# Fused attention backward: the core alternates dK with o, dQ and dV of two units, and the output projections move with it

## The chip, the core and the metric

The kernel runs on one core of one Trainium2 chip. Times are device microseconds (us) of one execution, medians over several. TensorE is called PE here, its weight loads PEld, VectorE DVE, ScalarE ACT, GpSimd POOL, and SyncE SP; "SPq" in a profile is SP's sequencer issuing DMAs. Nearly all DMAs of the part studied here are issued from SP, one after the other; I call that the sync queue.

## The reference, cut to what matters

The reference concatenates a linear-attention block and a multi-query attention block and returns the output and the gradients of all eight inputs and weights. The change concerns the attention block alone: sequence 2048, 16 heads of 28, one key and one value head shared by all.

```python
def _B_ref(x, wq, wk, wv, wo):
    q = (x @ wq).reshape(B, S, H, Dh) ...       # B=1, S=2048, H=16, Dh=28
    k = x @ wk;  v = x @ wv
    scores = jnp.einsum("bhqd,bkd->bhqk", q, k) * (Dh ** -0.5)
    p = _softmax(scores, axis=-1)
    o = jnp.einsum("bhqk,bkd->bhqd", p, v)
    return o....reshape(B, S, H * Dh) @ wo
...
_out, _vjp = jax.vjp(_f, ...);  _grads = _vjp(grad_out)
```

## The kernel before

After a first phase (the linear-attention block and projections, to about 245 us) comes a loop of 512 units. A unit is 256 queries by two heads by 256 keys. Eight units make a block (all 2048 keys, for 256 queries and two heads), eight blocks make one turn of 64 units (256 queries, all 16 heads). In unit `u` PE makes the scores S of unit `u` and the gradient products dP of unit `u - 16` (`w`); ACT takes two exponentials (`sp` to `eT`) and one copy of half of dP; DVE and POOL make dS (`dsT`), DVE a 32x32 transpose of it (`dsx`). From these PE accumulates o, dQ (both in the bank `oq`), dK and dV.

dV needs the exponentials with keys and queries exchanged. For that each pair of units issues one DMA transpose of 128x2048 bf16 (`eN<-eT`) on the sync queue. At the end of a block the o of two heads is transposed back on PE and normalised into `onat`. At the end of a turn `onat` is written to `on_d`, one more DMA transpose makes `oTq` of it, and two output projections multiply it by `wo`.

```python
psS = ...tile_pool(name="psS", bufs=3, PSUM)     # score banks, in rotation
psD = ...tile_pool(name="psD", bufs=2, PSUM)
...
def out_proj(i):
    ps = psS.tile([P, 512], F32, name="sps")
    for c in range(4):
        mm(ps[:, 0:D], oTq[i // 2][:, 4 * (i % 2) + c, :], wo[:, c, :], ...)
    ot = flat(R3)[:, 5120:5120 + D]               # one staging buffer
    nc.vector.tensor_copy(out=ot, in_=ps[:, 0:D])
    nc.sync.dma_start(out0[i * P:(i + 1) * P, D:2 * D], ot)
...
for u in range(NU + 28):                          # NU = 512
    if u == 14 or u % 64 == 32 and u < 448:       # qX: 16 DMAs of 64 KB
        for a in range(4):
            for B in range(4):
                nc.sync.dma_start(qx[32 * a:32 * a + 32, B, :, :], qn_d[r0:r0 + 64, :]...)
    ...
    rows_SD(u, sp, dp)                            # S and dP, tiles of 32 x 128
    nc.scalar.activation(out=et[:, u % 2, 0, :], in_=sp[0][:, :], func=ACT.Exp, ...)
    ...                                           # dS on DVE; cp on ACT; dS on POOL
    nc.scalar.activation(out=et[:, u % 2, 1, :], in_=sp[1][:, :], func=ACT.Exp, ...)
    if u % 2 == 1:
        nc.sync.dma_start_transpose(en[:, :, :], et...)                # eN<-eT
    ...                                           # block end, u = 8b+9: transposes into a bank of psS
    # six units of eight: 2 or 3 dK steps, tiles of 32 x 32
    # every unit: o of unit u-1 and dQ of unit u-18, tiles of 128 x 32
    # two units of eight: dV
    ...
    if u % 64 == 1 and u > 1:
        nc.sync.dma_start_transpose(oTq[q_][:, :, :], onat[q_]...)     # unit 65
    if u % 64 in (16, 24) and u > 64:
        out_proj(2 * (u // 64 - 1) + u % 64 // 8 - 2)                  # units 80 and 88
    ...
    if 0 <= y < NU and y % 8 == 7:                # dQ eviction, on ACT
        nc.scalar.activation(out=qT_B[g]..., in_=oq[64:128, 0:256], func=ACT.Copy, scale=scale)
```

## Time and profile before

| kernel before | value |
|---|---|
| median (lowest to highest), first three runs | 1175.03 us (1173.59 to 1176.06) |
| span of the profiled run | 1172.0 us |
| the loop, first score to last exponential | about 245 to 1091 us |
| one block; a block with an output projection | 12.78 us; 13.75 us |
| one turn of 64 units | 104.17 us |

The last two rows are differences between start times of the first exponential (line 710) in ACT's timeline. The page opens with each engine's busy time and share of the span:

```profile
PE 1099.7 (94%) x15388; PEld 444.6 (38%) x15388; DVE 885.5 (76%) x1669; ACT 900.9 (77%) x1788; POOL 699.4 (60%) x835
...
PEclk9999998989999999999999999999999999999999
```

The second line is the clock granted to PE, in tenths over 40 slices of the span; 9 means 90% or more. PE looks like the bound with 94%. But this share does not say what sets the pace of a unit, so units are read one by one. ACT's timeline (start, duration, engine, line, operation, output and input) of parts of two units:

```profile
465.56 0.60 ACT L710 ACTIVATE eT<-sps 128x512 bf16<-128x512 f32 x1
466.05 0.59 ACT L717 ACTIVATE cp<-dps 128x512 bf16<-128x512 f32 x1
466.53 0.61 ACT L720 ACTIVATE eT<-sps 128x512 bf16<-128x512 f32 x1
467.01 0.61 ACT L710 ACTIVATE eT<-sps 128x512 bf16<-128x512 f32 x1
...
468.63 0.38 ACT L847 ACTIVATE R_63<-oq 64x256 bf16<-64x256 f32 x1
469.04 0.60 ACT L710 ACTIVATE eT<-sps 128x512 bf16<-128x512 f32 x1
```

One unit is 1.45 us from first exponential to first exponential: three instructions, each starting 0.49 us after the one before, although each lasts 0.6. There ACT is full. The next unit takes 2.03 us: its block-end transposes had taken a score bank, and the dQ eviction (L847) sits in it. In a block of eight, six units take 1.46 to 1.55 us, one 2.03 and one 1.81.

The second thing to read is the sync queue, which no engine's busy share shows. Its timeline, at two places:

```profile
420.56 9.12 SPq L699 DMA_DIRECT2D qX<-qn_d  x16
429.79 5.70 SPq L723 DMA_TRANSPOSE eN<-eT  x2
...
475.48 1.80 SPq L723 DMA_TRANSPOSE eN<-eT  x1
477.37 1.12 SPq L750 DMA_DIRECT2D on_d<-onat  x1
478.54 1.94 SPq L838 DMA_TRANSPOSE oTq<-onat  x1
480.58 18.62 SPq L723 DMA_TRANSPOSE eN<-eT  x7
```

Each row begins where the one before it ended: SP issues without a pause. The sixteen loads of a qX take 9.1 us of it; eN transposes take 2.66 to 2.85 us each when they follow each other (18.62 us for seven, 5.70 for two). The Trainium skill, page Perfetto Trace Analysis, What "DMA-bound" means, lists an issuing sequencer whose track is solid DMA slices as one way to be DMA-bound, beside busy DMA engines. Here the view by stretches shows both: the packets make up 0.54 of the DMA engines' time while the sixteen loads are issued (420.5 to 429.7 us, 144 GB/s), but 1.21 and 1.16 in the stretches of transposes after it (184 and 191 GB/s; packets overlap, so the sum can pass 1). From 283 to 824 us there is hardly a gap. So an eN transpose is issued late: comparing each issue with the end of the exponential that completes its eT, the lag is 0 to 15 us, jumps by about 9 us at every qX load and is worked off until the next.

The oTq transpose at 478.54 belongs to unit 129 (unit 65 of the cut: the second of its turn), whose first exponential is at 467.01 us. Its reader, the projection of unit 144, is at 491.93 us, so nobody waits. The view of everything that touches the tile oTq says the same, in the line of what ended the idle time of its readers: only "issue", no DMA.

```profile
L79 PE MATMUL sps<-wo,oTq x64: 352/353/363, 387.8 to 1129.8; 128*128 128x448 bf16 x64
L838 SPq DMA_TRANSPOSE oTq<-onat x8: 1291/1298/1960, 374.4 to 1095.8; - x8
its engine sat idle before it (us, times) until:
  issue: 3.2, 15
```

### The profile page before, as it was taken

What the parts mean: (1) busy time and instruction counts of PE and PEld (TensorE: products, weight loads), DVE (VectorE), ACT (ScalarE), POOL (GpSimd) and SP (SyncE); (2) the same over time, 40 slices, a digit from 0 to 9 for tenths busy, and PEclk for the clock granted to TensorE, in tenths of its full rate; (3) what the DMA queues carried; (4) which work ended last, traced back from release to release, by engine and by line L of the source; (5) the groups of instructions that cost most, each with busy time, mean ns of one, the idle gap of its engine ahead of it and who ended that gap; (6) DMA issues with size and microseconds to landing.
All of it is one profiled execution on the core that took longest, in us unless ns stands there. A gap on an engine that the chain in (4) does not pass through costs nothing. (4 is left out here: it accounts for less than half of the span.)

```text
span 1172.0 us, 38434 instructions
## 1 busy us (share of the span) xinstructions
PE 1099.7 (94%) x15388; PEld 444.6 (38%) x15388; DVE 885.5 (76%) x1669; ACT 900.9 (77%) x1788; POOL 699.4 (60%) x835
## 2 busy tenths in 40 slices
PE   7999997988989999999999999999999999999998
PEld 4555543333333333333333333333333333333344
DVE  7886400336889898888889888988999899888922
ACT  3453112357989999999999999999999999999511
POOL 9000150003777777777778777877787778777900
PEclk9999998989999999999999999999999999999999
DMA  9779897059999999999999999999999999999962
GB/s 259 126 130 184 160 188 177 20 125 198 180 179 190 188 164 187 190 184 175 189 188 160 199 188 186 162 198 188 152 195 182 189 170 199 184 168 163 240 147 75
DMA packets 684435, 202.91 MB, mean 173 GB/s; under 512 B 651232, under 2 KB 679392, under 8 KB 684256
## 3 DMA queue, kind: packets, MB, share of 16 engines
q1 hardware_dynamic: 673664, 190.26, 94.8%
q10 hardware_dynamic: 9312, 6.65, 2.1%
q0 software_dynamic: 1280, 3.55, 1.1%
q8 instruction: 120, 1.97, 0.7%
q14 instruction: 59, 0.48, 0.1%
HBM read 22.83 MB, written 15.03 MB: 32 GB/s over the span
## 5 line engine op out<-in xcount | busy, mean ns | idle before, releaser
L718 POOL TENSOR_TENSOR dsT<-cp,eT 128x512 bf16<-128x512 bf16 x512 | 590.3, 1153 | 193.2 <-ACT cp L717 156.2
L715 DVE TENSOR_TENSOR dsT<-dps,eT 128x512 bf16<-128x512 f32 x512 | 347.8, 679 | 58.3 <-PE dps L591 37.6
L853 DVE STREAM_TRANSPOSE dsx<-dsT 128x512 f32<-128x512 f32 x512 | 357.8, 699 | 1.3 <-POOL dsT L718 0.3
L710 ACT ACTIVATE eT<-sps 128x512 bf16<-128x512 f32 x512 | 307.3, 600 | 42.2 <-PE dps L591 28.3
L591 PEld LDWEIGHTS <-R_65 32*128 32x128 bf16 (+1 forms) x8192 | 171.5, 92 | 403.3 <-issue 356.1
L717 ACT ACTIVATE cp<-dps 128x512 bf16<-128x512 f32 x512 | 305.1, 596 | 12.0 <-PE dps L591 11.1
L720 ACT ACTIVATE eT<-sps 128x512 bf16<-128x512 f32 x512 | 311.6, 609 | 0.0
L591 PE MATMUL dk_acc<-dsx,qX 32*32 32x512 bf16 x4096 | 290.4, 377 | 0.0
L591 PE MATMUL dps<-doT,R_65 32*128 32x256 bf16 x2048 | 253.9, 271 | 7.7 <-DVE R_64 L824 1.1
L591 PE MATMUL sps<-R_63,R_65 32*128 32x256 bf16 x2048 | 242.9, 276 | 5.9 <-ACT eT L710 2.0
L591 PE MATMUL oq<-eT,R_65 128*32 128x256 bf16 x2048 | 213.8, 278 | 2.5 <-issue 0.3
L591 PE MATMUL oq<-dsT,R_65 128*32 128x256 bf16 x2048 | 203.1, 278 | 1.1 <-POOL dsT L718 0.9
L591 PEld LDWEIGHTS <-qX 32*32 32x32 bf16 x4096 | 69.4, 89 | 94.1 <-issue 54.1
L591 PE MATMUL dv_acc<-eN,don 128*32 128x512 bf16 x1024 | 86.9, 382 | 2.5 <-DMA eN<-eT 2.5
L521 DVE TENSOR_TENSOR osb<-R_65 32x512 bf16<-32x512 bf16 x4 | 1.7, 413 | 74.2 <-ACT R_65 L518 74.2
L380 POOL MEMSET ga<- 64x448 bf16 x2 | 0.9, 468 | 90.8 <-PE agen L337 71.3
L553 POOL MEMSET R_65<- 128x16 bf16 x1 | 0.2, 172 | 70.8 <-DVE R_65 L552 70.8
L748 POOL TENSOR_TENSOR don<-R_64,rl 128x128 bf16<-128x128 bf16 x64 | 25.8, 403 | 21.4 <-DVE rl L740 21.4
L844 DVE COPY oTs<-oq 64x256 f32<-64x256 f32 x64 | 26.5, 414 | 15.1 <-PE oq L591 14.4
L731 PE MATMUL sps<-identF,oTs 64*128 64x64 f32 x128 | 21.3, 247 | 17.0 <-DVE oTs L844 10.6
L591 PEld LDWEIGHTS <-don 128*32 128x32 bf16 x1024 | 34.7, 97 | 4.0 <-issue 3.9
L79 PEld LDWEIGHTS <-R_64 128*128 128x128 bf16 x256 | 23.9, 100 | 28.0 <-issue 10.3
(216 smaller groups left out, 961.2 us busy)
## 6 DMA issues: line engine op xcount, KB each, us to landing
qX<-qn_d SPq DMA_DIRECT2D x128, 64.0 KB
out_dram<-osb ACTq DMA_DIRECT2D x44, 112.0 KB
eN<-eT SPq DMA_TRANSPOSE x256
qn_d<-dsx SPq DMA_DIRECT2D x1, 2048.0 KB
on_d<-onat SPq DMA_DIRECT2D x8, 256.0 KB
xa<-in_A_x_dram SPq DMA_DIRECT2D x8, 224.0 KB
ga<-in_grad_out_dram SPq DMA_DIRECT2D x4, 448.0 KB
xa<-in_grad_out_dram POOLq DMA_DIRECT2D x4, 448.0 KB, 4.7
```

The source lines that it names most:

```text
L79: nc.tensor.matmul(out_ap, lhsT=lhsT, rhs=rhs, start=start, stop=stop, tile_position=(0, 0))
L521: nc.vector.tensor_tensor(out=sq[0:32, :], in0=kT[0:32, qc * 512:(qc + 1) * 512], in1=kT[0:32, qc * 512:(qc + 1) * 512], op=ALU.mult)
L591: nc.tensor.matmul(out, lhsT=lhsT, rhs=rhs, start=start, stop=stop, tile_position=pos, skip_group_check=True)
L710: nc.scalar.activation(out=et[:, u % 2, 0, :], in_=sp[0][:, :], func=ACT.Exp, scale=scale)
L715: nc.vector.tensor_tensor(out=dst[:, 0, :], in0=dp[0][:, :], in1=ew[:, w % 2, 0, :], op=ALU.mult)
L717: nc.scalar.activation(out=cp[:, :], in_=dp[1][:, :], func=ACT.Copy)
L718: nc.gpsimd.tensor_tensor(out=dst[:, 1, :], in0=cp[:, :], in1=ew[:, w % 2, 1, :], op=ALU.mult)
L720: nc.scalar.activation(out=et[:, u % 2, 1, :], in_=sp[1][:, :], func=ACT.Exp, scale=scale)
L731: nc.tensor.transpose(onp[:, qb, :, :].rearrange("p h c -> p (h c)"), oTs[b][0:64, qb * P:(qb + 1) * P], identF[0:64, 0:64], tile_position ...
L748: nc.gpsimd.tensor_tensor(out=dn[:], in0=dnv, in1=r_[:].to_broadcast([P, 2, 2, 32]), op=ALU.mult)
L844: nc.vector.tensor_copy(out=oTs[v // 8][:, :], in_=oq[0:64, 0:256])
L853: nc.vector.transpose(out=dsx[b][:, tp, :, :, :].rearrange("p h t c -> p (h t c)").bitcast(F32), in_=dsT[y][:, :, :].rearrange("p h c -> p ...
```

## The change

The intent is fewer changes of tiling on PE. Before, PE goes through S and dP (tiles of 32x128), dK (32x32), o and dQ (128x32) in most units. After, odd units have S, dP and dK; even units have S, dP, and the o, dQ and dV of two units. With it: the PSUM banks are named by hand, so that block-end transposes and projections take `spare`, the bank of the next unit's first scores; the dQ eviction moves from ACT to DVE; `wo` is loaded later into a freed region; and the output projections move from units 80 and 88 to units 68 and 76, while the oTq transpose they read is issued in unit 66 instead of 65. Cut to its core:

```diff
-        psS = ...(name="psS", bufs=3, PSUM);  psD = ...(name="psD", bufs=2, PSUM)
+        SB = [psA.tile([P, 512], F32, name=f"sps{i}") for i in range(3)]
+        DB = [psA.tile([P, 512], F32, name=f"dps{i}") for i in range(2)]
...
+                sp = [SB[(2 * u + h) % 3] for h in range(2)] if hasS else None
+                spare = SB[(2 * u + 2) % 3]
                 rows_SD(u, sp, dp)
+                if (b := due(u, 10)) is not None:      # due: u is lag units after block b began
+                    onat_T(b, spare)
+                if (b := due(u, 14)) is not None:
+                    don_T(b, spare)
+                if u % 64 in (4, 12) and u > 64:
+                    out_proj(u, spare)
...
+                if (b := due(u, 10)) is not None:
+                    o_norm(b)
+                    do_o(b)
+                    if b % 8 == 7:
+                        nc.sync.dma_start_transpose(oTq[q_][:, :, :], onat[q_]...)
+                if u % 64 in (4, 12) and u > 64:
+                    out_store(u, spare)
...
-                x = u - 28                              # dK in six units of eight
...
-                    # o of unit u-1 and dQ of unit u-18 in every unit; dV in two of eight
+                if u % 2:
+                    b, i = divmod(u - 27, 8)
+                    if 0 <= b < NB:
+                        for m in range(2 * i, 2 * i + 4):
+                            dk_m(b, m)
+                else:
+                    o_dq((u - 2, u - 1), (u - 20, u - 19))
+                    if (b := due(u, 20)) is not None:
+                        dv_mm(b, 0)
+                    if (b := due(u, 24)) is not None:
+                        dv_mm(b, 1)
...
-                if u % 64 in (16, 24) and u > 64:
-                    out_proj(2 * (u // 64 - 1) + u % 64 // 8 - 2)
...
-                    nc.scalar.activation(out=qT_B[g]..., in_=oq[64:128, 0:256], func=ACT.Copy, scale=scale)
+                    nc.vector.tensor_scalar(out=qT_B[g]..., in0=oq[64:128, 0:256], scalar1=scale, ...)
```

Two pools get a buffer more each (eN 12, dsT 5), and three small tiles get fewer (`oTs` and `prod` one, `doT` two). Some block-end steps move by a unit: the transposes of o, for one, from unit 9 after the block's start to unit 10.

More of the change, by code (lines that the diff above doesn't have):

```diff
@@ L571 @@
     with ExitStack() as cs_:
-        psS = psc.enter_context(tc.tile_pool(name="psS", bufs=3, space=bass.MemoryType.PSUM))
-        psD = psc.enter_context(tc.tile_pool(name="psD", bufs=2, space=bass.MemoryType.PSUM))
         psA = psc.enter_context(tc.tile_pool(name="psAcc", bufs=1, space=bass.MemoryType.PSUM))
         pe_ = cs_.enter_context(tc.tile_pool(name="ceT", bufs=10, side="right"))
-        pn_ = cs_.enter_context(tc.tile_pool(name="ceN", bufs=11, side="right"))
-        pd_ = cs_.enter_context(tc.tile_pool(name="cdsT", bufs=4, side="right"))
+        pn_ = cs_.enter_context(tc.tile_pool(name="ceN", bufs=12, side="right"))
+        pd_ = cs_.enter_context(tc.tile_pool(name="cdsT", bufs=5, side="right"))
         px_ = cs_.enter_context(tc.tile_pool(name="cdsx", bufs=2, side="right"))
@@ L624, with out_proj, out_store @@
         make_identity(nc, identF[:])
-        wo = pp_.tile([P, 4, D], BF16, name="wo", bufs=1)
-        nc.sync.dma_start(wo[:, :, :], wo_d[:, 0:D].rearrange("(g p) c -> p g c", p=P))
+        wo = R4[:, :, 0:D]
         oTq = {}
-        def out_proj(i):
-            ps = psS.tile([P, 512], F32, name="sps")
+        def out_proj(u, ps):
+            i = 2 * (u // 64 - 1) + u % 64 // 8
             for c in range(4):
                 mm(ps[:, 0:D], oTq[i // 2][:, 4 * (i % 2) + c, :], wo[:, c, :], start=(c == 0), stop=(c == 3))
+        def out_store(u, ps):
+            i = 2 * (u // 64 - 1) + u % 64 // 8
             ot = flat(R3)[:, 5120:5120 + D]
@@ L676, in gwo @@
                 if st == 0:
-                    post["acc"] = psS.tile([P, 512], F32, name="sps")
+                    post["acc"] = SB[g_ % 3]
                 al = post["acc"]
@@ L686, in gwo, with due, onat_T @@
                         nc.sync.dma_start(out_8[h * DH:(h + 1) * DH, :], sb[32 * j + 1:32 * j + 1 + DH, :])
+        onps, tps2 = {}, {}
+        def due(u, lag):
+            b, r = divmod(u - lag, 8)
+            return b if r == 0 and 0 <= b < NB else None
+        def onat_T(b, bank):
+            onp = bank[:, 0:P].rearrange("p (q h c) -> p q h c", q=2, h=2)
+            for qb in range(2):
+                nc.tensor.transpose(onp[:, qb, :, :].rearrange("p h c -> p (h c)"),
+                                    oTs[b][0:64, qb * P:(qb + 1) * P], identF[0:64, 0:64],
+                                    tile_position=(0, 0))
+            onps[b] = onp
@@ new lines, in o_norm @@
+        def o_norm(b):
+            onp = onps.pop(b)
+            qc, pair, g, hp = blk(b)
+            if pair == 0:
+                onat[qc] = pm_.tile([P, 2, 512], BF16, name="onat")
+            ont = onat[qc]
+            cs0 = slice(pair * 64, pair * 64 + 64)
+            r_ = pw_.tile([P, 2, 2, 1], F32, name="rl")
+            nc.vector.reciprocal(out=r_[:], in_=onp[:, :, :, 0:1])
+            rl[b] = r_
+            onv = ont[:, :, cs0].rearrange("p q (h c) -> p q h c", c=32)
+            dnv = do_nat[:, 2 * qc:2 * qc + 2, cs0].rearrange("p q (h c) -> p q h c", c=32)
+            nc.vector.tensor_tensor(out=onv, in0=onp[:, :, :, :], in1=r_[:].to_broadcast([P, 2, 2, 32]),
+                                    op=ALU.mult)
+            dn = pw_.tile([P, 2, 2, 32], BF16, name="don")
+            don[b] = dn
+            nc.gpsimd.tensor_tensor(out=dn[:], in0=dnv, in1=r_[:].to_broadcast([P, 2, 2, 32]), op=ALU.mult)
+            if pair == 7:
+                nc.sync.dma_start(on_d[qc * 256:(qc + 1) * 256, :].rearrange("(q p) c -> p q c", p=P),
+                                  ont[:, :, :])
@@ new lines, in do_o, with row_D @@
+        def do_o(b):
+            qc, pair, g, hp = blk(b)
+            prod[b] = pw_.tile([P, 2, 2, 32], F32, name="prod", bufs=1)
+            nc.gpsimd.tensor_tensor(
+                out=prod[b][:],
+                in0=do_nat[:, 2 * qc:2 * qc + 2, pair * 64:pair * 64 + 64].rearrange("p q (h c) -> p q h c", c=32),
+                in1=onat[qc][:, :, pair * 64:pair * 64 + 64].rearrange("p q (h c) -> p q h c", c=32),
+                op=ALU.mult)
+        def row_D(b):
+            Dq = pw_.tile([P, 2, 2, 1], F32, name="Dq")
+            nc.vector.tensor_reduce(out=Dq[:, :, :, 0], in_=prod[b][:], axis=AX.X, op=ALU.add)
+            nc.gpsimd.tensor_tensor(out=don[b][:, :, :, 0:1], in0=Dq[:], in1=rl[b][:], op=ALU.mult)
@@ new lines, in don_T, with don_copy @@
+        def don_T(b, bank):
+            r = 64 * (1 - b % 2)
+            tp2 = bank[:, 0:P].bitcast(BF16)
+            for qb in range(2):
+                nc.tensor.transpose(tp2[r:r + 64, qb * P:(qb + 1) * P],
+                                    don[b][:, qb, :, :].rearrange("p h c -> p (h c)"), identB[:, :],
+                                    tile_position=(0, r))
+            tps2[b] = tp2
+        def don_copy(b):
+            r = 64 * (1 - b % 2)
+            doT[b] = pw_.tile([P, 256], BF16, name="doT", bufs=2)
+            nc.vector.tensor_copy(out=doT[b][r:r + 64, :], in_=tps2.pop(b)[r:r + 64, 0:256])
@@ new lines, in dk_m @@
+        def dk_m(b, m):
+            qc, pair, g, hp = blk(b)
+            h, B, s = m // 8, (m // 2) % 4, m % 2
+            for a in range(4):
+                rhs = dsx[b][32 * a:32 * a + 32, :, h, :, :].rearrange(
+                    "p u t (b i s) -> p u t b i s", b=4, s=2)[:, :, :, B, :, s]
+                mmt(dk_acc[32 * a:32 * a + 32, :],
+                    qX[qc][32 * a:32 * a + 32, B, s, pair * 64 + 32 * h:pair * 64 + 32 * h + 32],
+                    rhs, (32 * a, 32 * a), b == 0 and m == 0, b == NB - 1 and m == 15)
@@ new lines, in o_mm, with dq_mm @@
+        def o_mm(v):
+            b, tp = divmod(v, 8)
+            for t2 in range(2):
+                t = 2 * tp + t2
+                for h in range(2):
+                    mmt(oq[32 * h:32 * h + 32, 0:256], vaug[:, t, :],
+                        eT[v // 2][:, v % 2, h, t2 * 256:(t2 + 1) * 256], (0, 32 * h), t == 0, t == 15)
+                yield
+        def dq_mm(y):
+            b, tp = divmod(y, 8)
+            for t2 in range(2):
+                t = 2 * tp + t2
+                for h in range(2):
+                    mmt(oq[64 + 32 * h:96 + 32 * h, 0:256], kn[:, t, :],
+                        dsT[y][:, h, t2 * 256:(t2 + 1) * 256], (0, 64 + 32 * h), t == 0, t == 15)
+                yield
@@ new lines, in o_dq, with dv_mm @@
+        def o_dq(vs, ys):
+            for v, y in zip(vs, ys):
+                todo = [f(i) for f, i in ((o_mm, v), (dq_mm, y)) if 0 <= i < NU]
+                for _ in range(2):
+                    for g_ in todo:
+                        next(g_)
+        def dv_mm(b, h):
+            for qb in range(2):
+                for c in range(4):
+                    rhs = eN[4 * b + c][:, :, :].rearrange("p (u h t q) k -> p u h t q k", u=2, h=2,
+                                                           t=2)[:, :, h, :, qb, :]
+                    mmt(dv_acc[32 * c:32 * c + 32, :], don[b][:, qb, h, :], rhs, (0, 32 * c),
+                        b == 0 and h + qb == 0, b == NB - 1 and h + qb == 2)
@@ L701 @@
                     qX[qc] = qx
-                sp = [psS.tile([P, 512], F32, name="sps") for _ in range(2)] if hasS else None
-                dp = [psD.tile([P, 512], F32, name="dps") for _ in range(2)] if hasD else None
-                rows_SD(u, sp, dp)
+                if u == 20:
+                    nc.sync.dma_start(wo, wo_d[:, 0:D].rearrange("(g p) c -> p g c", p=P))
+                sp = [SB[(2 * u + h) % 3] for h in range(2)] if hasS else None
+                dp = DB if hasD else None
+                spare = SB[(2 * u + 2) % 3]
+                rows_SD(u, sp, dp)
+                if (b := due(u, 10)) is not None:
[4 more added lines that the diff above has]
+                    out_proj(u, spare)
                 if hasS:
@@ L718 @@
                     nc.gpsimd.tensor_tensor(out=dst[:, 1, :], in0=cp[:, :], in1=ew[:, w % 2, 1, :], op=ALU.mult)
+                if (b := due(u, 10)) is not None:
+                    o_norm(b)
+                    do_o(b)
+                    if b % 8 == 7:
+                        q_ = b // 8
+                        oTq[q_] = pp_.tile([P, 8, P], BF16, name="oTq", bufs=1)
+                        nc.sync.dma_start_transpose(oTq[q_][:, :, :], onat[q_][:, :, :].rearrange("p q c -> p (q c)"))
+                if (b := due(u, 14)) is not None:
+                    don_copy(b)
+                if u % 64 in (4, 12) and u > 64:
+                    out_store(u, spare)
                 if hasS:
@@ L724 @@
                         eN[u // 2] = en
-                e = u - 9
-                if e >= 0 and e % 8 == 0 and e // 8 < NB:
-                    b = e // 8
-                    onp = psS.tile([P, 2, 2, 32], F32, name="sps")
-                    for qb in range(2):
-                        nc.tensor.transpose(onp[:, qb, :, :].rearrange("p h c -> p (h c)"),
-                                            oTs[b][0:64, qb * P:(qb + 1) * P], identF[0:64, 0:64],
-                                            tile_position=(0, 0))
-                    qc, pair, g, hp = blk(b)
-                    if pair == 0:
-                        onat[qc] = pm_.tile([P, 2, 512], BF16, name="onat")
-                    ont = onat[qc]
-                    cs0 = slice(pair * 64, pair * 64 + 64)
-                    r_ = pw_.tile([P, 2, 2, 1], F32, name="rl")
-                    nc.vector.reciprocal(out=r_[:], in_=onp[:, :, :, 0:1])
-                    rl[b] = r_
-                    onv = ont[:, :, cs0].rearrange("p q (h c) -> p q h c", c=32)
-                    dnv = do_nat[:, 2 * qc:2 * qc + 2, cs0].rearrange("p q (h c) -> p q h c", c=32)
-                    nc.vector.tensor_tensor(out=onv, in0=onp[:, :, :, :], in1=r_[:].to_broadcast([P, 2, 2, 32]),
-                                            op=ALU.mult)
-                    dn = pw_.tile([P, 2, 2, 32], BF16, name="don")
-                    don[b] = dn
-                    nc.gpsimd.tensor_tensor(out=dn[:], in0=dnv, in1=r_[:].to_broadcast([P, 2, 2, 32]), op=ALU.mult)
-                    if pair == 7:
-                        nc.sync.dma_start(on_d[qc * 256:(qc + 1) * 256, :].rearrange("(q p) c -> p q c", p=P),
-                                          ont[:, :, :])
@@ L752 @@
-                e = u - 10
-                if e >= 0 and e % 8 == 0 and e // 8 < NB:
-                    b = e // 8
-                    qc, pair, g, hp = blk(b)
-                    prod[b] = pw_.tile([P, 2, 2, 32], F32, name="prod")
-                    nc.gpsimd.tensor_tensor(
-                        out=prod[b][:],
-                        in0=do_nat[:, 2 * qc:2 * qc + 2, pair * 64:pair * 64 + 64].rearrange(
-                            "p q (h c) -> p q h c", c=32),
-                        in1=onat[qc][:, :, pair * 64:pair * 64 + 64].rearrange("p q (h c) -> p q h c", c=32),
-                        op=ALU.mult)
@@ L763 @@
-                e = u - 12
-                if e >= 0 and e % 8 == 0 and e // 8 < NB:
-                    b = e // 8
-                    Dq = pw_.tile([P, 2, 2, 1], F32, name="Dq")
-                    nc.vector.tensor_reduce(out=Dq[:, :, :, 0], in_=prod[b][:], axis=AX.X, op=ALU.add)
-                    nc.gpsimd.tensor_tensor(out=don[b][:, :, :, 0:1], in0=Dq[:], in1=rl[b][:], op=ALU.mult)
-                e = u - 14
-                if e >= 0 and e % 8 == 0 and e // 8 < NB:
-                    b = e // 8
-                    qc, pair, g, hp = blk(b)
-                    r = 64 * (1 - hp)
-                    tp2 = psS.tile([P, 1024], BF16, name="sps")
-                    for qb in range(2):
-                        nc.tensor.transpose(tp2[r:r + 64, qb * P:(qb + 1) * P],
-                                            don[b][:, qb, :, :].rearrange("p h c -> p (h c)"), identB[:, :],
-                                            tile_position=(0, r))
-                    doT[b] = pw_.tile([P, 256], BF16, name="doT")
-                    nc.vector.tensor_copy(out=doT[b][r:r + 64, :], in_=tp2[r:r + 64, 0:256])
@@ L782 @@
-                x = u - 28
-                if 0 <= x and x // 8 < NB and x % 8 < 6:
-                    b = x // 8
-                    qc, pair, g, hp = blk(b)
-                    m0 = 3 * (x % 8) - max(0, x % 8 - 4)
-                    for m in range(m0, m0 + (3 if x % 8 < 4 else 2)):
-                        h, B, s = m // 8, (m // 2) % 4, m % 2
-                        for a in range(4):
-                            rhs = dsx[b][32 * a:32 * a + 32, :, h, :, :].rearrange(
-                                "p u t (b i s) -> p u t b i s", b=4, s=2)[:, :, :, B, :, s]
-                            mmt(dk_acc[32 * a:32 * a + 32, :],
-                                qX[qc][32 * a:32 * a + 32, B, s, pair * 64 + 32 * h:pair * 64 + 32 * h + 32],
-                                rhs, (32 * a, 32 * a), b == 0 and m == 0, b == NB - 1 and m == 15)
+                if u % 2:
[9 more added lines that the diff above has]
+                        dv_mm(b, 1)
@@ L796 @@
                 v = u - 1
                 y = u - 18
-                for t2 in range(2):
-                    if 0 <= v < NU:
-                        b, tp = divmod(v, 8)
-                        t = 2 * tp + t2
-                        for h in range(2):
-                            mmt(oq[32 * h:32 * h + 32, 0:256], vaug[:, t, :],
-                                eT[v // 2][:, v % 2, h, t2 * 256:(t2 + 1) * 256], (0, 32 * h), t == 0, t == 15)
-                    if 0 <= y < NU:
-                        b, tp = divmod(y, 8)
-                        t = 2 * tp + t2
-                        for h in range(2):
-                            mmt(oq[64 + 32 * h:96 + 32 * h, 0:256], kn[:, t, :],
-                                dsT[y][:, h, t2 * 256:(t2 + 1) * 256], (0, 64 + 32 * h), t == 0, t == 15)
@@ L811 @@
-                if u >= 18 and u % 8 in (2, 3) and (u - 18) // 8 < NB:
-                    b, h = divmod(u - 18, 8)
-                    for qb in range(2):
-                        for c in range(4):
-                            rhs = eN[4 * b + c][:, :, :].rearrange("p (u h t q) k -> p u h t q k", u=2, h=2,
-                                                                   t=2)[:, :, h, :, qb, :]
-                            mmt(dv_acc[32 * c:32 * c + 32, :], don[b][:, qb, h, :], rhs, (0, 32 * c),
-                                b == 0 and h + qb == 0, b == NB - 1 and h + qb == 2)
@@ L820 @@
-                if v < NS and v >= 0:
-                    ps = psD.tile([P, 512], F32, name="dps")
+                if 0 <= v < NS:
+                    ps = DB[v % 2]
                     for c in range(4):
@@ L827 @@
                     post_load((u - 512) // 2)
-                if u == 530:
+                if u == 531:
                     dqn = px_.tile([P, 8, 2, 2, 256], BF16, name="dsx").rearrange("p a b c d -> p (a b c d)").rearrange(
@@ L834 @@
                     gwo(6 * (u - 530), min(64, 6 * (u - 529)))
-                if u % 64 == 1 and u > 1:
-                    q_ = u // 64 - 1
-                    oTq[q_] = pp_.tile([P, 8, P], BF16, name="oTq", bufs=1)
-                    nc.sync.dma_start_transpose(oTq[q_][:, :, :], onat[q_][:, :, :].rearrange("p q c -> p (q c)"))
-                if u % 64 in (16, 24) and u > 64:
-                    out_proj(2 * (u // 64 - 1) + u % 64 // 8 - 2)
-                if 0 <= v < NU and v % 8 == 7:
-                    oTs[v // 8] = pm_.tile([64, 256], F32, name="oTs")
-                    nc.vector.tensor_copy(out=oTs[v // 8][:, :], in_=oq[0:64, 0:256])
-                if 0 <= y < NU and y % 8 == 7:
-                    qc, pair, g, hp = blk(y // 8)
-                    nc.scalar.activation(out=qT_B[g][64 * hp:64 * hp + 64, qc * 256:(qc + 1) * 256],
-                                         in_=oq[64:128, 0:256], func=ACT.Copy, scale=scale)
                 if 0 <= y < NU:
@@ L855 @@
                         in_=dsT[y][:, :, :].rearrange("p h c -> p (h c)").bitcast(F32))
+                if (b := due(u, 11)) is not None:
+                    row_D(b)
+                if (b := due(u, 8)) is not None:
+                    oTs[b] = pm_.tile([64, 256], F32, name="oTs", bufs=1)
+                    nc.vector.tensor_copy(out=oTs[b][:, :], in_=oq[0:64, 0:256])
+                if (b := due(u, 26)) is not None:
+                    qc, pair, g, hp = blk(b)
+                    nc.vector.tensor_scalar(out=qT_B[g][64 * hp:64 * hp + 64, qc * 256:(qc + 1) * 256],
+                                            in0=oq[64:128, 0:256], scalar1=scale, scalar2=None, op0=ALU.mult)
         gwo(60, 64)
@@ L859 @@
         dkvn = post["dkvn"].rearrange("p (t c) -> p t c", c=64)
+        gens = [0, 0]
         def gen(i, dt=F32):
-            return [psS, psD][i % 2].tile([P, 512], dt, name=["sps", "dps"][i % 2])
+            gens[i % 2] += 1
+            t = [SB, DB][i % 2][gens[i % 2] % (3 - i % 2)]
+            return t.bitcast(dt) if dt != F32 else t
         def sbuf():
@@ L880 @@
         for q4 in range(4):
-            ps = gen(1, BF16).rearrange("p (s k) -> p s k", k=P)
+            ps = gen(1, BF16)[:, 0:512].rearrange("p (s k) -> p s k", k=P)
             for s in range(4):
```

## The prediction

> **What bounds it now.** The main loop (512 units in 64 blocks of 8, about 245 to 1091 us of a 1172 us span) repeats exactly. By start times of the first exponential (ACT's timeline): 12.78 us a block, 13.75 us in the two blocks of eight with an output projection, 104.15 us per 64 units. Most units take 1.46 us: ACT's three evictions at 0.485 us start to start. The excess, 1.1 us a block, sits in two units (2.03 and 1.81 us) whose block-end transposes take a score bank, so that the next scores wait for the second exponential; the longer one also has the dQ copy on ACT.
>
> Unseen in the engines' busy shares, the sync queue is full too. Its timeline shows hardly a gap from 283 to 824 us. Each eN transpose takes 2.85 us of it, 32 of them 91 us; the qX load adds 9.2 us per 64 units, the rest 3.2: 103.5 of 104.15 us. An eN transpose is issued 0 to 15 us after its eT is ready: the lag jumps by 9 us at each qX load, then is worked off. The oTq transpose, in the same queue, is issued 6 to 10 us late and lands 4 to 5 us later; its projection stands 15 units on and doesn't notice.
>
> **What the change does.** It takes changes of tiling away. The page TensorEngine Tiling (Array Packing), Key Properties, says that changing the mode drains the engine; here a group of matmuls pays about 0.11 us above its streaming time (8 dK matmuls 0.54 us, 12 take 0.76). 22 changes a block become 16: about 0.7 us of PE. The dQ copy goes to DVE (0.35 us; DVE then has 11.25 us a block, ACT 11.64). DVE, not ACT, frees the transposes' bank. By itself the loop would come to 11.9 us a block, 97.4 us per 64 units.
>
> **Why I expect no gain.** The queue still needs 103.5 us. And the projections move from units 80 and 88 to 68 and 76, while oTq's transpose is issued at unit 66. PE works in order, so at unit 68 it waits until the queue has worked off its lag, transposed oTq and landed it: about 10 us, eight times. Then the queue runs dry for some 4 us and only follows compute until the next qX load. The period becomes about 108 us; and the idle spell brings the halved clock (page TensorE: Matmul & The Clock Gate, HAM oscillation: idle over some 3.4 us throttles; this trace has 0.50 from 297 to 300 us), another 2 us.
>
> **Sum.** First wait: +14 us. Six periods at +4 to +6: +30. Last period, without qX: -7. Tail, one more wait: +3. Total +41: 1216 us. Range 1190 to 1245. Faster by over 2%: 0.05; within: 0.10; slower: 0.85.
>
> **What would show it.** Waits: PE's weight load of oTq held by the DMA, eight times, 5 to 20 us each. Unit times between: 1.46 to 1.55 us, no 2.03. Period 107 to 112 us. PE's clock below 1 after each wait. Gaps in the sync queue after each. Last exponential near 1130 us, not 1091.
>
> **What would make it wrong.** If the queue catches up before unit 66, its 103.5 us alone bounds: 1150 to 1160 us. If DVE's added work (1.97 us in the unit with normalisation and dQ eviction) slows units, it is slower still; if the clock stays up, 1200 us.

## The result, and the profile after

| | before | after |
|---|---|---|
| median (lowest to highest), 4 runs each | 1174.31 us (1172.84 to 1176.06) | 1221.82 us (1217.84 to 1225.77) |
| span of the profiled run | 1172.0 us | 1216.1 us |
| block without a wait | 12.78 us | 12.25 us |
| turn of 64 units | 104.17 us | 109.9 us |
| last exponential ends | 1091.0 us | 1130.7 us |

The ratio is 1.0405, 95% interval 1.0377 to 1.0432: 4% slower. Here and below a ratio compares the fast runs of two kernels from the same rounds; it is not quite the ratio of the medians quoted. All outputs are correct.

The units did become faster; the turn became longer. The page's shares:

```profile
PE 1069.1 (88%) x15379; PEld 487.8 (40%) x15388; DVE 903.3 (74%) x1733; ACT 875.0 (72%) x1724; POOL 700.7 (58%) x835
...
PEclk9999998986997999999899989989998999999899
```

PE's share fell from 94 to 88%, and the clock dips at regular distances. The tile view of oTq now names a DMA, 16 times (eight waits of the weight load, and the matmul behind it, which counts the same stretch again):

```profile
L79 PE MATMUL sps<-R,oTq x64: 352/458/581, 376.3 to 1155.3; 128*128 128x448 bf16 x64
L841 SPq DMA_TRANSPOSE oTq<-onat x8: 1282/1290/2117, 372.6 to 1136.1; - x8
its engine sat idle before it (us, times) until:
  DMA oTq<-onat: 141.2, 16
```

The view of waits (engine, line, what it waited for: us in total, times, the longest) counts them once for the weight load:

```profile
PEld L79 <- DMA oTq<-onat: 71.7, 8, 13.7
```

Eight waits, 71.7 us together. The sync queue around one of them:

```profile
475.29 5.85 SPq L850 DMA_TRANSPOSE eN<-eT  x2
481.24 0.62 SPq L721 DMA_DIRECT2D on_d<-onat  x1
481.90 1.29 SPq L841 DMA_TRANSPOSE oTq<-onat  x1
483.30 2.45 SPq L850 DMA_TRANSPOSE eN<-eT  x1
487.94 0.36 SPq L637 DMA_DIRECT2D out_dram<-R  x1
491.10 8.09 SPq L850 DMA_TRANSPOSE eN<-eT  x3
```

Until 483.30 the rows follow each other as before. Then the queue stands idle from 485.75 to 487.94 and from 488.30 to 491.10, 5.0 us: PE waits for oTq, so no new scores, no new exponentials, and nothing to transpose. The chain of waits through this place, in order of time (start, us, what), ties the two together:

```profile
479.05 0.50 ACT eT L847
479.55 1.60 SPq L850
...
481.24 0.62 SPq L721
481.90 3.58 DMA oTq<-onat
...
485.52 1.68 PE sps L79 x4
487.20 0.97 PE oq L591 x13
...
489.03 0.33 PE sps L591 x2
```

The exponentials end, SP finishes the eN transposes ahead in the queue, stores on_d, transposes oTq (3.58 us from issue to landing), and only then PE projects. Unit 69's scores stand behind the projection in PE's program, and PE did not start them before it. There is a second cost, PE's clock. The view by stretches gives start and end, length, the busy us of PE, PEld, DVE, ACT and POOL (with counts), then the granted clock, the DMA share and GB/s:

```profile
477.90:485.50 7.60, 0.08 (x2) 0.00 (x0) 1.01 (x3) 1.57 (x3) 1.93 (x3) 0.80 1.01 212
485.50:489.40 3.90, 3.88 (x36) 1.34 (x37) 1.24 (x2) 0.00 (x0) 0.00 (x0) 0.52 0.59 123
489.40:500.00 10.60, 10.01 (x182) 4.32 (x180) 9.89 (x19) 10.50 (x21) 7.65 (x9) 1.00 0.75 132
```

The first row is the wait, in which PE works for 0.08 us of 7.60, the second the work just after it, at a clock of 0.52; in the third the clock is full again. PE's timeline compares the same work after the wait and in the second projection, eight units later:

```profile
485.52 1.68 PE L79 MATMUL sps<-R,oTq 128*128 128x448 bf16 x4 [7.55 <-DMA oTq<-onat]
...
488.96 0.39 PE L591 MATMUL sps<-R,R 32*128 32x256 bf16 x2
...
500.23 0.93 PE L79 MATMUL sps<-R,oTq 128*128 128x448 bf16 x4
...
502.08 0.28 PE L591 MATMUL sps<-R,R 32*128 32x256 bf16 x2
```

From the projection to the next scores it is 3.44 us (488.96 less 485.52) at the halved clock, against 1.85 us (502.08 less 500.23) at the full one: 1.6 us more. All seven pairs of the loop show it, with 1.4 to 1.6 us each, 10.9 us together. That agrees with the Trainium skill, page TensorE: Matmul & The Clock Gate, HAM oscillation, which says that an idle spell of more than about 3.4 us brings the halved clock back: PE sat idle for 5.1 us or more at each of the eight waits, and the trace has a clock of 0.50 after or within each. But a shorter spell was enough elsewhere: in e1_late_proj below, idle spells of 2.4 and 2.3 us (from 504.6 and 607.4 us) were followed by 0.50 for 3.4 us (from 508.2 and 610.6 us).

ACT's timeline answers to the one shown of before. The unit of 2.03 us is gone; the longest undisturbed one is now 1.77 us (476.19 to 477.96), and the next takes 11.54 us:

```profile
476.19 0.60 ACT L826 ACTIVATE eT<-sps 128x512 bf16<-128x512 f32 x1 [0.31 <-PE dps L591]
...
477.96 0.60 ACT L826 ACTIVATE eT<-sps 128x512 bf16<-128x512 f32 x1 [0.19 <-issue]
...
489.50 0.60 ACT L826 ACTIVATE eT<-sps 128x512 bf16<-128x512 f32 x1 [9.96 <-PE dps L591]
```

### The profile page after: what moved, and what is told of

It is laid out like the page before. It is cut to its first block, busy times and chain, and to the rows that moved or that the text cites. A ratio compares the mean times of both kernels' runs of the same rounds, so it can differ in the third digit from the quotient of the medians.

```text
span 1216.1 us, 38536 instructions
## 1 busy us (share of the span) xinstructions
PE 1069.1 (88%) x15379; PEld 487.8 (40%) x15388; DVE 903.3 (74%) x1733; ACT 875.0 (72%) x1724; POOL 700.7 (58%) x835
## 3 DMA queue, kind: packets, MB, share of 16 engines
q8 instruction: 120, 1.97, 0.6%
## 4 chain that ended last, share of the span: by engine, by line
PE 64%; DVE 17%; ACT 9%; DMA 5%; SPq 3%; issue 2%; POOL 0%; ACTq 0%; DVEq 0%; POOLq 0%
PE dk_acc L591 15%; PE agen L79 10%; PE oq L591 8%; PE dps L591 7%; PE sps L591 7%; DVE dsT L831 6%; PE dv_acc L591 5%; PE sps L79 5%; ACT eT L847 4%; DVE dsx L887 3%; ACT eT L826 3%; PE aacc L79 3%; DMA oTq<-onat 3%; DVE R L897 2%; PE dps L79 2%
## 5 line engine op out<-in xcount | busy, mean ns | idle before, releaser
L826 ACT ACTIVATE eT<-sps 128x512 bf16<-128x512 f32 x512 | 307.3, 600 | 114.9 <-PE dps L591 91.2
L591 PEld LDWEIGHTS <-R 32*128 32x128 bf16 (+1 forms) x8192 | 203.4, 94 | 324.8 <-issue 274.0
L591 PE MATMUL dps<-doT,R 32*128 32x256 bf16 x2048 | 255.7, 273 | 15.7 <-DVE dsT L831 14.5
L591 PE MATMUL dk_acc<-dsx,qX 32*32 32x512 bf16 x4096 | 269.3, 377 | 0.0
L591 PE MATMUL sps<-R,R 32*128 32x256 bf16 x2048 | 246.6, 279 | 18.5 <-ACT eT L826 4.4
L591 PE MATMUL oq<-eT,R 128*32 128x256 bf16 x2048 | 163.0, 283 | 0.0
L591 PE MATMUL oq<-dsT,R 128*32 128x256 bf16 x2048 | 162.6, 282 | 0.0
L591 PEld LDWEIGHTS <-qX 32*32 32x32 bf16 x4096 | 80.0, 89 | 114.7 <-issue 54.4
L79 PE MATMUL sps<-R,oTq 128*128 128x448 bf16 x64 | 20.8, 464 | 69.5 <-DMA oTq<-onat 69.5
L79 PEld LDWEIGHTS <-R 128*128 128x128 bf16 (+1 forms) x416 | 34.1, 99 | 36.3 <-issue 12.0
L719 POOL TENSOR_TENSOR don<-R,rl 128x128 bf16<-128x128 bf16 x64 | 26.0, 406 | 21.0 <-DVE rl L711 21.0
L79 PEld LDWEIGHTS <-oTq 128*128 128x128 bf16 x64 | 5.9, 114 | 78.4 <-DMA oTq<-onat 71.7
```

Of the source, the lines that this page charges most:

```text
L79: nc.tensor.matmul(out_ap, lhsT=lhsT, rhs=rhs, start=start, stop=stop, tile_position=(0, 0))
L591: nc.tensor.matmul(out, lhsT=lhsT, rhs=rhs, start=start, stop=stop, tile_position=pos, skip_group_check=True)
L719: nc.gpsimd.tensor_tensor(out=dn[:], in0=dnv, in1=r_[:].to_broadcast([P, 2, 2, 32]), op=ALU.mult)
```

## The experiments

The theory: the loss is PE's in-order wait for oTq, at a projection placed two units after the transpose was issued into a queue that is behind by several us. The rivals: the alternation or the hand-placed banks are slow in themselves; the wait is oTq's own latency and no backlog is involved; the queue bounded the kernel before already, so nothing could be gained.

| run | edit | median us (lowest to highest) | ratio to before [95%] | block / turn, us |
|---|---|---|---|---|
| e1_late_proj | after, projections at units 84, 92 | 1164.2 (1162.01 to 1168.98) | 0.9917 [0.989, 0.9945] | 12.25 / 103.0 |
| e2_before_early_proj | before, projections at units 68, 76 | 1236.8 (1231.82 to 1242.67) | 1.0532 [1.0492, 1.0572] | 12.78 / 112.5 |
| e3_qx4 | after, qX in four loads | 1196.09 (1192.87 to 1200.5) | 1.0186 [1.0155, 1.0217] | 12.25 / 107.1 |
| e4_late_qx4 | both edits | 1140.03 (1136.18 to 1144.02) | 0.9699 [0.9662, 0.9736] | 12.25 / 99.8 |
| e5_dq_on_act | e4, dQ eviction on ACT | 1148.54 (1147.06 to 1148.84) | 0.976 [0.9712, 0.9808] | 12.43 |
| e6_before_qx4 | before, qX in four loads | 1172.17 (1168.22 to 1174.19) | 0.9956 [0.9894, 1.0018] | 12.78 / 104.2 |
| e7_dq_later_ot2 | e4, dQ eviction a unit later, second staging buffer; WRONG in one output | 1162.48 (1160.67 to 1171.98) | 0.9897 [0.9835, 0.996] | 12.77 |
| e8_no_alternation | e4, order of matmuls as before | 1167.79 (1164.42 to 1168.89) | 0.9921 [0.9871, 0.9972] | 12.70 |
| e9_dq_after_next_ds | e4, dQ eviction early in the next unit, second staging buffer | 1139.79 (1134.81 to 1141.63) | 0.9696 [0.967, 0.9721] | 12.17 |
| e4_again | e4 beside e9 | 1144.39 (1135.03 to 1147.24) | 0.9722 [0.9689, 0.9755] | 12.26 |

Blocks and turns are again differences of the first exponential's start times; a turn is the mean of five.

### Only the projections later

```diff
-                if u % 64 in (4, 12) and u > 64:
+                if proj_at(u) is not None:       # units 84 and 92; 520 and 528 in the last turn
                     out_proj(u, spare)
```

> The changed kernel with only its two output projections moved from units 68 and 76 of each 64 to units 84 and 92 (520 and 528 in the last turn), so 18 units lie between the issue of oTq's transpose and its first reader. Theory (the loss is PE waiting at the projection for oTq behind the backlog of the sync queue): the eight waits of 5 to 14 us vanish, units stay at 12.2 us a block, and the queue's own 103.5 us per 64 units bounds the loop; about 1155 us (1145 to 1165), faster than before by 1 to 2.5%. Rival (the alternation, the hand-placed banks or the halved clock cost the time by themselves): 1200 us or more, with the time still lost in the loop.

Measured: 1164.2 us, 58 us less than the changed kernel, with all else of the change in place. Of the eight waits for oTq one is left, in the tail. So the alternation and the banks together do not cost the time, and the placement does. The loop's turn is 103.0 us, as the queue's own work had been summed up (103.5), and SP issues without a gap of 0.5 us or more from 281 to 1090 us: with the waits gone, the queue is the bound. Its lag shows in a second place, which I had not foreseen:

```profile
DVE R L640 <- DMA out_dram<-R: 15.1, 7, 3.8
...
PEld L79 <- DMA oTq<-onat: 3.1, 1, 3.1
```

The second projection reuses the one staging buffer, and DVE waits for the store of the first, which stands in the same queue. Through these waits, and four of PE for eN (4.9 us together), the queue holds the loop back.

### The kernel before, only the projections earlier

```diff
-                if u % 64 in (16, 24) and u > 64:
-                    out_proj(2 * (u // 64 - 1) + u % 64 // 8 - 2)
+                if u % 64 in (4, 12) and u > 64:
+                    out_proj(2 * (u // 64 - 1) + u % 64 // 8)
```

> The kernel before with only its two output projections moved from units 80 and 88 of each 64 to units 68 and 76; oTq's transpose stays at unit 65. Theory: eight waits of PE for oTq appear (7 to 12 us), the period of 64 units grows from 104.15 to about 111 us, time about 1230 us (1210 to 1245). Rival (the loss belongs to the alternation or the banks): within 1% of before, 1174 us.

Measured: 1236.8 us, 5% slower than before, with the units untouched at 12.78 us. Its view of waits:

```profile
PEld L79 <- DMA oTq<-onat: 50.7, 8, 9.5
```

The one edit makes the same eight waits in the old loop and costs more than the whole change did (the turn is 112.5 us, I had expected 111). This is the sharpest test: the loss belongs to the placement, whatever the order of the other matmuls.

### The changed kernel with a shorter queue

```diff
-                    for a in range(4):
-                        for B in range(4):
-                            r0 = qc * 256 + 64 * B
-                            nc.sync.dma_start(qx[32 * a:32 * a + 32, B, :, :],
-                                              qn_d[r0:r0 + 64, :].rearrange("(j s) c -> j s c", s=2))
+                    src = qn_d[qc * 256:(qc + 1) * 256, :].rearrange("(b j s) c -> j b (s c)", b=4, s=2)
+                    for a in range(4):
+                        nc.sync.dma_start(qx[32 * a:32 * a + 32, :, :, :].rearrange("p b s c -> p b (s c)"), src)
```

> The changed kernel with the sixteen loads of a qX issued as four with the same bytes, so that the sync queue gives them 2 to 3 us instead of 9.2 per 64 units. Theory (each wait is the lag of the queue at unit 66 plus about 4 us for oTq itself): the lag at unit 66 falls from 6 us to 0 to 2, the wait from 8.5 to about 4 to 5 us, the period from 109.7 to 105 us; about 1182 us (1168 to 1195). Rival (the wait is oTq's own time from issue to landing and has nothing to do with a backlog): waits of 8 us as in the changed kernel, over 1210 us.

Measured: 1196.09 us, 14 us more than expected and just outside the range. The four loads take 3.40 us of the queue here, the longest of eight times (the shortest is 1.75), for the same bytes that take 9.61 in the changed kernel (7.30 to 9.98):

```profile
PEld L79 <- DMA oTq<-onat: 50.9, 8, 11.3
...
423.55 3.40 SPq L805 DMA_DIRECT2D qX<-qn_d  x4
427.06 7.49 SPq L848 DMA_TRANSPOSE eN<-eT  x2
```

The same place in the changed kernel:

```profile
424.38 9.61 SPq L806 DMA_DIRECT2D qX<-qn_d  x16
434.11 1.80 SPq L850 DMA_TRANSPOSE eN<-eT  x1
```

The direction is the theory's: a shorter backlog, 21 us less waiting, 26 us less time. The size is smaller than I thought. One reason shows in the traces: the eN transpose right after the loads now takes 4.5 to 5.9 us, where it took 1.3 to 3.1. From the first load to the start of the second transpose behind it, the queue is on average 3.4 us shorter per turn (7.7 against 11.0 us), not the 6 us that the loads alone suggest. After the first (11.3 us) each wait is 5.2 to 6.1 us instead of 4 to 5. The second of them can be taken apart. Normalisation ends at 474.96 us, an eN transpose issued just before holds the queue until 477.64, on_d takes 0.91 us, oTq is issued at 478.70, and PE, idle since 477.20, starts the projection at 482.22. Without the transpose in the way PE would still have waited for about 2.3 us, by an estimate from these times; the other 2.7 us are backlog. So the wait has two parts, backlog and oTq's own way through the queue; only a later reader removes both. Theory and rival are both half right here, and moving the projection settles it.

### Both edits

> The changed kernel with both edits: late projections and four qX loads. Theory: the queue now needs 97 to 100 us per 64 units, about what the units themselves take (7 blocks of 12.25 and one of about 13 and 13: 99.6), so the loop is bound by the units; about 1138 us (1128 to 1150). If the queue with late projections alone is not the bound, this is the same as the run with late projections alone.

Measured: 1140.03 us, 3% faster than before, and 1144.39 in a second set of runs. The turn is 99.8 us, what the units take by themselves (six blocks of 12.25 us and two of 13.0 give 99.5). The queue is just as full: SP has no gap of 0.5 us or more from 283 to 1070 us, so both limits lie together here. This is 24 us below the run with late projections alone, so the queue was that one's bound.

### The four loads in the kernel before

> The kernel before with only the four qX loads. Theory: its units, not the queue, set its 104.15 us per 64 units, so it stays there; only the wait for eN of 3 us near 336 us goes: 1166 to 1174, 0 to 0.8% faster. Rival (the queue bounded the kernel before): the gain is that of the queue, about 4 us per 64 units, 1145 us or less.

Measured: 1172.17 us, ratio 0.9956 with an interval that includes 1; the turn stays 104.2 us. Before the change the units set the pace and the queue only just kept up. Neither change alone is worth much: shorter units without a shorter queue give 0.8% (projections late), a shorter queue without shorter units 0.4%, which is within the noise, both 3%.

### Parts of the change, on the run with both edits

There a longer unit shows, so that parts can be weighed (a shorter one need not, because the queue is full too). First the dQ eviction back on ACT:

```diff
-                    nc.vector.tensor_scalar(out=qT_B[g]..., in0=oq[64:128, 0:256], scalar1=scale, ...)
+                    nc.scalar.activation(out=qT_B[g]..., in_=oq[64:128, 0:256], func=ACT.Copy, scale=scale)
```

> The run with late projections and four qX loads (1140 us), with the dQ eviction alone put back on ACT. Its own worth: ACT gets 0.3 us back in the unit that ends a dQ, DVE loses 0.35 there. Theory: the unit of 1.77 us (DVE late after its 1.97 us of work) goes back to about 1.5 and the one before grows by about 0.3, so a block stays at 12.25 +- 0.1 and the time within 0.5% of 1140. If moving dQ to DVE was what shortened the block from 12.78, the block is 12.5 or more and the time 1155 or more.

Measured: 1148.54 us, ratio 0.976, beside 1140.03 and 1144.39 us (0.9699 and 0.9722) of the two runs with both edits, which are of other sets; a block of 12.43 us. The unit of 1.77 us went back to 1.51 and the one before grew from 1.56 to 2.00. The expectation (12.15 to 12.35 us, within 0.5% of 1140) is missed, by little: the unit before grew by more than the next one shrank. By the blocks of the profile the move to DVE is worth 0.18 us a block; the intervals of the times overlap.

Then the order of the matmuls as before (dV in units 2 and 3 of a block, dK in six units, o and dQ in every unit, the dQ eviction one unit earlier accordingly):

```diff
-                if u % 2:
-                    ... dk_m of four steps
-                else:
-                    o_dq((u - 2, u - 1), (u - 20, u - 19)) ... dv_mm
+                x = u - 28
+                ... dk_m of three or two steps in six units of eight
+                o_dq((u - 1,), (u - 18,))
+                if (b := due(u, 18)) is not None: dv_mm(b, 0)
+                if (b := due(u, 19)) is not None: dv_mm(b, 1)
```

> The 1140 us run with the order of matmuls put back: dK and o, dQ of one unit in each unit, as before, all else kept (banks, dQ on DVE, late projections, four qX loads). Theory: 22 group changes a block instead of 16 cost PE 0.7 us, which shows only in the units where PE is then the longest (those with transposes or dV): a block of about 12.5, 1152 us. If the alternation is worth nothing, 1140; if it is the whole gain over before, a block of 12.8 and 1172.

Measured: 1167.79 us and a block of 12.70 us; I had expected 1152. The alternation is worth 0.45 us a block, nearly all of the 0.53 us between 12.78 and 12.25. With the 0.18 us of the dQ eviction the parts come to more than the whole, so they don't simply add up. A caveat: in this run the transposes of o and the first half of dV meet in one unit (1.90 us), which is partly a matter of placement. The Trainium skill, page TensorEngine Tiling (Array Packing), Key Properties, says that changing the tiling mode drains the engine; six changes fewer per block fit that, but no run here separates the drain from the placement.

### Shorter units still

> The 1140 us run with the dQ eviction one unit later (after the unit's own work on DVE) and a second staging buffer for the output rows. By units: the unit of 1.77 us falls to about 1.5, a block to about 12.0, which would be 1125 us. By the queue, which already has hardly a gap in the 1140 us run (about 100 us per 64 units): waits for eN come in its place and the time stays within 0.7% of 1140. I expect 1135.

This run is a miss twice. The last block's dQ was evicted after its transpose had been issued, so one output (the gradient of `wq`) is wrong; and it is slower, 1162.48 us. The unit of 1.77 us did fall to 1.51, but PE waited at the next dQ group instead, because dQ's bank was freed too late:

```profile
PE oq L591 <- DVE R L899: 41.2, 48, 2.9
```

The next run evicts dQ at the start of the next unit's DVE work, right after its dS, and is correct.

> The 1140 us run with two changes: the dQ eviction stays on DVE but comes in the next unit, right after that unit's dS, so that the dQ matmuls of the unit after find their bank free (the run that put it at the end of that unit made PE wait 0.75 us a block), and a second staging buffer for the output rows. By units: 1.77 us becomes about 1.55, a block 12.0 to 12.05, and the loop alone would be 13 us shorter, 1127. By the queue: the 1140 us run has no gap in it through the loop, so its 100 us per 64 units stand, the last eN transpose is issued at about 1059 us as there, and only the lag grows: 1133 to 1140, within 0.6%. I expect the queue to win: 1137.

> The same kernel as the 1140 us run, beside the run above on one chip, so that under 1% can be told: 1140 us, 3% under before.

Measured on one chip: 1139.79 us against 1144.39 us, ratios to before 0.9696 [0.967, 0.9721] and 0.9722 [0.9689, 0.9755]. The intervals overlap, so the two are not told apart. A block is 0.1 us shorter (12.17 against 12.26; the unit after took part of the gain), and the last exponential ends 5 us earlier in the profile (1047.8 against 1052.7 us). But the last eN transpose is issued at 1054.0 in the one and at 1054.4 us in the other, and both queues are without a gap of 0.5 us or more until 1064 us. The lag at the first transpose of a turn grows from 6.7 us in the second turn to 10.3 in the last with the shorter block; in the two profiles of the 1140 us kernel it goes from 4.0 to 9.7 and from 4.8 to 4.7 us. Equal last issues and a growing lag are what a queue-bound loop would show; no run shortened the queue further to prove it.

## Why the prediction was right

The time was put at 1216 us, range 1190 to 1245, slower by over 2% with 0.85; it is 1221.82 us. Step by step, with start times of unit 69's exponential in the turns:

| term | predicted | measured, after less before |
|---|---|---|
| first wait | +14 us | 380.3 less 369.3: +11.0 |
| six turns | +4 to +6 each, +30 | 109.87 less 104.18 each: +34.1 |
| last turn, no qX | -7 | 91.2 less 96.6: -5.4 |
| tail | +3 | 85.4 less 81.0: +4.4 |
| sum | +41 (rounded terms: +40) | +44.1 (1216.1 less 1172.0) |

- *The queue's load and lag.* Right: 103.5 us per turn were predicted, 103.0 measured where it is the bound.
- *PE waits at unit 68, eight times, 5 to 20 us each.* Right: 5.4 to 13.7 us, 71.7 us together; the six between the first and the last are 7.8 to 9.5 us, 8.8 on average, where about 10 were forecast. Putting the projections back into late units removed them, putting them early in the old kernel made them.
- *The queue runs dry for some 4 us after each wait.* Right: 5.0 us at the place shown.
- *The clock.* Predicted 2 us per wait, measured 1.4 to 1.6. The half clock that the prediction names in the kernel before, from 297 to 300 us, is no example of it: PE had been busy for 2.60 of the 3.40 us just before, with no idle spell over 0.6 us.
- *The turn becomes 108 us, with the clock 110.* Measured 109.9.
- *Units between waits 1.46 to 1.55 us, no 2.03; the loop by itself 97.4 us per turn.* Half right. The 2.03 and 1.81 us units went, but a unit of 1.77 us appeared, and the block is 12.25 us, not 11.9; a turn without waits takes 99.5 us. The term that was too small is DVE's delay in the unit with normalisation and dQ eviction, 1.97 us of work against 1.46 us of unit. The prediction named it under what could make it wrong, and left it out of the sum. That the turn was still right within 0.1 us is luck in part: 99.6 us of units, 8.8 of wait and 1.6 of clock make 110.0, where 97.4, about 10 and 2 had been thought of. In the same way the terms of the table miss by -3.0, +4.1, +1.6 and +1.4 us, and partly cancel.
- *If the waits vanish, 1150 to 1160 us.* Measured 1164.2, a little above. The seven waits for the staging buffer, 15.1 us together, had not been foreseen.

What stays open: how much of the alternation's gain is the drain at a change of tiling and how much is placement; the cost of the halved clock apart from the wait, which was read from seven pairs of projections and not tested by a run; and whether issuing or the DMA engines behind it make a transpose last 2.85 us in the full queue.

## What to carry to other kernels

When work on an in-order engine is moved earlier, look up where its operands come from, and how late that source really is: for a DMA, compare the issue time in the trace with the time its data was ready, not the program's order. A DMA queue that is hardly ever idle can be the bound although no engine's share says so. Whether it is, is told by shortening it: in the kernel before that changed nothing clear of noise, with the projections late it gave 24 us. A reader placed close behind it turns its lag into idle time of the whole pipeline. Two bounds that lie within 1% of each other (104.17 us of units, 103.5 us of queue) have to be lifted together: each edit alone gave under 1%, both gave 3%.

## What the Trainium skill lacked or had wrong

- DMA: Bandwidth & Descriptors, Latency and other measured facts, gives 261 GB/s for a DMA transpose with a non-contiguous middle dimension and about 350 to 400 GB/s for a contiguous one. Here a transpose of 128x2048 bf16 (524,288 bytes) from SBUF to SBUF takes about 2.85 us of a full queue, which is 184 GB/s; the view by stretches gives 184 and 191 GB/s for all DMAs there.
- The same page, Issuing engines are not separate DMA queues, calls the time to initiate a DMA usually small relative to the DMA. The sixteen loads of 64 KB here took 7.3 to 10.5 us of the issuing queue in a row, about 0.55 us each, while the DMA engines moved less than afterwards (144 GB/s against 184). The same bytes in four loads took 1.75 to 3.5 us; the next transpose then took about 3 us longer, so 3.4 us a turn remained. In the changed kernel this alone was worth 26 us, and 24 us with the projections late.
- TensorEngine Tiling (Array Packing), Key Properties, says that changing the tiling mode drains the engine and gives no cost. Here 8 dK matmuls take 0.54 us to the start of the next group and 12 take 0.76, which makes 0.055 us each and 0.10 us besides for the group (an estimate from these two, and not a measured drain), and six changes fewer per block, with their placement, 0.45 us.
